# A state-space convolution followed by a gated FFN: per-block sums of spectrum products, a quadrant tap filter with token-major v, an in-place norm, and a new order of all instructions

## The chip, the cores and the metric

The kernel runs on one core of a Trainium2 chip. The metric is the device time of one execution in microseconds, and the median of the runs is compared.

## What is computed

Two layers on 2048 tokens of 640 features. The first normalizes q, filters k with four taps, multiplies by v, convolves the product causally with a 2048-long filter for each feature (given through an FFT), adds a skip term and gates by q. The second normalizes again and applies a gated FFN of width 1728.

```python
def _A_ref(q, k, v, shift_k, ssm_k, ssm_D):
    k_pad = jnp.pad(k, ((0, 0), (ks - 1, 0), (0, 0)))
    k_shift = sum over t of k_pad[:, t:t + S, :] * shift_k[:, ks - 1 - t]
    kv = k_shift * v
    y = irfft(rfft(kv, 2 * S) * rfft(ssm_k, 2 * S))[:S]      # along the tokens
    y = y + kv * ssm_D
    return q * y

def _B_ref(x, w_gate, w_up, w_down):
    return (silu(x @ w_gate) * (x @ w_up)) @ w_down

h = A_q + _A_ref(_layernorm(A_q), A_k, A_v, A_shift_k, A_ssm_k, A_ssm_D)
out = h + _B_ref(_layernorm(h), B_w_gate, B_w_up, B_w_down)
```

Shapes: S = 2048, D = 640, F = 1728, bfloat16 in and out.

## The kernel before

The tokens are cut into four blocks of 512. The long convolution is done block by block in a spectrum of 512 points: four blocks of the filter are transformed once into `C[0]` to `C[3]`, each block i of kv is transformed into `XH`, and the spectrum `Y[i]` of output block i is the sum of the products of input block j with filter block i - j, for j from 0 to i.

For each token block i the stages are:

- `kvload` and `kv`: k and v are brought in feature-major by transposing DMAs on SP's queue (`kT`, `vT`). For each chunk of 128 features TensorE adds up four taps with diagonal 128x128 weights (`diag`, L551). VectorE multiplies the PSUM result by `vT` (L557), and five more transposing DMAs bring the product token-major into `kvo`.
- `xfwd`: 32 matmuls against the table `ftab` (L516), evictions on ScalarE (L522), butterflies on VectorE (`bfly`, L504) into `XH`.
- `prod(j, i)`: on VectorE, two halves of two 2560-wide products (L574, L576), a subtraction and an addition 1280 wide (L579, L581), and for j > 0 an addition into `Y[i]` (L584). As soon as `XH` of block j is there, its products with all filters that need it are due, so the four `Y` all live side by side.
- `ln1`: two statistics passes on ScalarE for each quarter of the block (L592, L595), and on GpSimd an addition of epsilon (L598) and a power of -1/2 (L600).
- `inverse`: matmuls against `itab` (L613) from `OS` and `Y`, evicted on ScalarE with the norm's scale (L621); VectorE multiplies by the centred q (L623) and adds q (L626). Statistics of the second norm on ScalarE (L628, L630) and GpSimd (L632, L634), the normalization on VectorE (L636), and a transposing DMA into `hnT`.
- `ffn`: 14 tiles of gate and up matmuls (L657, L658; the last is packed, L667), evictions on ScalarE (L673, L675), the gate product on VectorE (L677), the down projection (L693), the residual on VectorE (L704) and the output DMA.

`ktrans` (L489, L494) and `kfwd` make the filter spectra from `kc`, with a table `ktab` of their own. The weights `GA`, `UA`, `GB`, `UB`, `PK`, `Wd` are loaded once.

Every operation is a task of a `_Graph`. `schedule` walks through time with a cost for each task and picks for each engine the ready task with the lowest key; the keys of the stages are in the table `ORDER`, limits hold the PSUM units in use by each class (four units of two banks). `emit` writes each engine's list in that order, with semaphore waits for the dependences, so on the chip each engine runs a fixed list, in order.

Of the kernel before, what the change touches and what calls it, by code (L numbers as in the profile page):

```python
# [12 lines left out]
P = 128  # L13
LN_EPS = 1e-5
CELL = 32

# [5 lines left out]
class _Task:  # L22
    __slots__ = ("eng", "fn", "cost", "lat", "prio", "deps", "raw", "succ", "npred", "ready", "end",
                 "opens", "tiles", "idx", "clock", "sem", "seq", "nbytes", "after", "key")


class _Pr:

    def __init__(self, key, base, off=0):
        self.key, self.base, self.off = key, base, off  # L30

    def __add__(self, n):
        return _Pr(self.key, self.base, self.off + n)

    def on(self, eng, table):
        return table.get((eng, self.key), self.base) + 0.01 * self.off
# [28 lines left out]
class _Graph:  # L65

    def __init__(self, nc, es, units=4):
        self.nc = nc
        self.es = es
        self.tasks = []  # L70
        self.lastw = {}
        self.readers = {}
        self.units = units
        self.ps = es.enter_context(nc.psum_tensor("ps", [P, 4096], dt.float32))
        self.psb = self.ps[:].bitcast(dt.bfloat16)
        self.order = None
# [26 lines left out]
    def add(self, eng, fn, cost, prio, r=(), w=(), pr=(), pw=(), skip=(), lat=None, nbytes=0, after=()):  # L103
        t = _Task()
        t.eng, t.fn, t.cost, t.prio = eng, fn, cost, prio
        t.lat = lat if lat is not None else {"pe": 200, "act": 190, "dve": 117, "pool": 110, "sp": 2000}[eng]
        t.nbytes = nbytes
        t.deps, t.raw = set(), set()
        t.after = set(after)
        t.opens = None  # L110
        t.tiles = []
        t.seq = len(self.tasks)
        for ap in r:
            for c in self.cells(ap):
                q = self.lastw.get(c)
                if q is not None:
                    t.deps.add(q)
                    t.raw.add(q)
                self.readers.setdefault(c, set()).add(t)
        for ap in w:  # L120
            for c in self.cells(ap):
                q = self.lastw.get(c)
                if q is not None and q is not t:
                    t.deps.add(q)
                    t.raw.add(q)
# [13 lines left out]
        for pt in pr:  # L139
            t.deps.update(pt.writers)  # L140
            t.raw.update(pt.writers)
            pt.users.append(t)
            t.tiles.append(pt)
        t.deps.discard(t)
        t.raw.discard(t)
        for s in skip:
            t.deps.discard(s)
            t.raw.discard(s)
# [3 lines left out]
    def schedule(self, limits, table):  # L152
        self.limits = limits
        for t in self.tasks:
            t.succ = []
            t.ready = 0.0
        for t in self.tasks:
            t.key = t.prio.on(t.eng, table) if isinstance(t.prio, _Pr) else t.prio
            t.npred = len(t.deps | t.after)
            for d in t.deps | t.after:  # L160
                d.succ.append(t)
        engs = ("pe", "act", "dve", "pool", "sp")
        free = {e: 0.0 for e in engs}
        cand = {e: [] for e in engs}
        for t in self.tasks:
            if t.npred == 0:
                cand[t.eng].append(t)
        unit_free = [0.0] * self.units
        unit_by = [None] * self.units
        used = {}  # L170
        left = {}
        self.last_users = {}
        dma_free = 0.0
        order = {e: [] for e in engs}
        glob = []
        total = len(self.tasks)
        while len(glob) < total:
            best = None
            for e in engs:
                cs = cand[e]  # L180
                if not cs:
                    continue
                open_at = None
                if e == "pe":
                    fu = [u for u in range(self.units) if unit_by[u] is None]
                    open_at = min((unit_free[u] for u in fu), default=None)
                lst = []
                for t in cs:
                    a = t.ready
                    if t.opens is not None:  # L190
                        if open_at is None or used.get(t.opens.cls, 0) >= limits.get(t.opens.cls, 99):
                            continue
                        a = max(a, open_at)
                    lst.append((a, t))
                if not lst:
                    continue
                at = max(free[e], min(x[0] for x in lst))
                a, t = min((x for x in lst if x[0] <= at + 1e-6), key=lambda x: (x[1].key, x[1].seq))
                if best is None or at < best[0]:
                    best = (at, e, t)  # L200
            assert best is not None, "schedule stuck"
            at, e, t = best
            cand[e].remove(t)
            if t.opens is not None:
                pt = t.opens
                fu = [u for u in range(self.units) if unit_by[u] is None and unit_free[u] <= at + 1e-6]
                u = min(fu, key=lambda x: unit_free[x])
                pt.unit = u
                used[pt.cls] = used.get(pt.cls, 0) + 1
                left[pt] = len(pt.users)  # L210
                prev = self.last_users.get(u, ())
                t.deps.update(prev)
                unit_by[u] = pt
            free[e] = at + t.cost
            t.end = at + t.cost + t.lat
            if e == "sp" and t.nbytes:
                dma_free = max(dma_free, at + t.cost) + t.nbytes / 340.0
                t.end = dma_free + t.lat
            for pt in t.tiles:
                left[pt] -= 1  # L220
                if left[pt] == 0:
# [3 lines left out]
                    used[pt.cls] -= 1  # L225
                    self.last_users[u] = [x for x in pt.users if x.eng != "pe"]
            for s in t.succ:
                s.npred -= 1
                s.ready = max(s.ready, t.end)
                if s.npred == 0:  # L230
                    cand[s.eng].append(s)
            order[e].append(t)
            t.idx = len(order[e])
            glob.append(t)
        self.order = order
        self.glob = glob
        return max(t.end for t in glob)

    def emit(self, block):
        nc, es = self.nc, self.es  # L240
        sems = {e: es.enter_context(nc.semaphore("s_" + e)) for e in ("pe", "act", "dve", "pool")}
        known = {e: {} for e in ("pe", "act", "dve", "pool", "sp")}
        prog = {e: [] for e in known}
        nd = 0
        for t in self.glob:
# [3 lines left out]
            for d in t.deps:  # L249
                if d.eng == t.eng == "pe":  # L250
                    continue
                key = d.sem if d.eng == "sp" else d.eng
                val = 16 if d.eng == "sp" else d.idx
# [14 lines left out]
            if t.eng == "sp":  # L268
# [3 lines left out]
                prog["sp"].append(lambda e, t=t: t.fn(e).then_inc(t.sem, 16))  # L272
# [3 lines left out]
        for t in self.glob:  # L276
            if t.eng == "sp" and not t.succ:
# [36 lines left out]
    ("dve", "kv0"): 134.7, ("dve", "kv1"): 333.2, ("dve", "kv2"): 36.6, ("dve", "kv3"): 580.7, ("dve", "mul"): 41.9,  # L314
    ("dve", "p00"): 463.5, ("dve", "p01"): 572.5, ("dve", "p02"): 151.9, ("dve", "p03"): 92.4, ("dve", "p11"): 542.8,
    ("dve", "p12"): 631.7, ("dve", "p13"): 91.9, ("dve", "p22"): 92.9, ("dve", "p23"): 668.8, ("dve", "p33"): 92.9,
    ("dve", "res"): 154.9, ("dve", "xf0"): 584.2, ("dve", "xf1"): 579.6, ("dve", "xf2"): 135.2, ("dve", "xf3"): 758.2,
# [468 lines left out]
```

## Time and profile before

The three runs shown took 302.02, 303.7 and 306.11 us; the median is 303.7.

| | |
|---|---|
| span of the profiled execution | 301.8 us |
| TensorE matmul busy | 264.4 us (88%) |
| VectorE busy | 221.2 us (73%) |
| ScalarE busy | 174.0 us (58%) |
| GpSimd busy | 54.6 us (18%) |
| mean granted TensorE clock | 0.970 |
| moved by DMA | 26.91 MB |
| chain that ended last | TensorE 50%, VectorE 28%, ScalarE 12% |

The span runs from the first to the last instruction of the profiled execution. The page names no other time of that execution; the median of the runs is 1.9 us above its span. Busy time is the union of an engine's instructions; the mean of one instruction includes its overlap with the next on the same engine.

### The profile page before, as it was taken

To read this page: it belongs to the slowest core of one execution; us is meant where nothing else is said; L and a number is where in the kernel's file an instruction comes from. 1 tells how busy PE (TensorE), PEld (TensorE's weight loads), DVE (VectorE), ACT (ScalarE), POOL (GpSimd) and SP (SyncE) were. 2 spreads that over 40 slices of the span, in tenths; PEclk is the share of its full clock that TensorE was granted. 3 is DMA by queue.
4 is the path that set the end of the run, shared out by engine and by line. 5 is a ranking of instruction groups with operands and counts; after the bars stand their busy time and mean duration, and the time that the engine had idled before them with its cause. 6 is when DMAs were issued, how large, how long until landed. Compare 5 with 4: busy or idle time off the path is not lost.

```text
span 301.8 us, 3881 instructions
## 1 busy us (share of the span) xinstructions
PE 264.4 (88%) x1515; PEld 144.5 (48%) x1532; DVE 221.2 (73%) x274; ACT 174.0 (58%) x330; POOL 54.6 (18%) x46
## 2 busy tenths in 40 slices
PE   1889879081789999989999999979999999999995
PEld 1556434050234555646445456644445564544563
DVE  3170898988999999999999999899998322212122
ACT  1749999239674764083289843848959803254400
POOL 0000000305279000015000493630301300000000
PEclk9999998867799999999999999999999999999999
DMA  5999891968445015104301200161000250000011
GB/s 171 249 364 218 219 281 21 239 177 213 83 89 174 0 37 124 50 13 87 109 25 31 57 2 22 34 131 77 0 2 1 48 85 22 11 13 0 0 46 43
DMA packets 55076, 26.91 MB, mean 89 GB/s; under 512 B 45265, under 2 KB 54162, under 8 KB 55058
## 3 DMA queue, kind: packets, MB, share of 16 engines
q1 hardware_dynamic: 55058, 26.67, 35.5%
q8 instruction: 12, 0.20, 0.3%
q14 instruction: 6, 0.05, 0.1%
HBM read 13.49 MB, written 2.62 MB: 53 GB/s over the span
## 4 chain that ended last, share of the span: by engine, by line
PE 50%; DVE 28%; ACT 12%; DMA 3%; POOL 3%; SPq 2%; issue 1%
PE ps L658 13%; PE ps L693 13%; PE ps L657 12%; DVE tt L574 5%; PE ps L516 4%; PE ps L613 4%; DVE Y L584 3%; DVE tt L576 3%; ACT KT L494 3%; PE ps L551 2%; DVE xh L704 2%; POOL mv L632 2%; DVE kT L557 2%; DVE tt L581 2%; ACT qo L630 2%; SPq L447 2%
## 5 line engine op out<-in xcount | busy, mean ns | idle before, releaser
L673 ACT ACTIVATE gu<-ps 128x512 bf16<-128x512 f32 (+1 forms) x56 | 33.4, 599 | 55.6 <-PE ps L658 52.3
L693 PE MATMUL ps<-Wd,gu 128*128 128x320 bf16 x448 | 64.9, 299 | 0.1
L658 PE MATMUL ps<-hnT,UA 128*128 128x512 bf16 x140 | 53.1, 379 | 2.7 <-DMA hnT<-qo 2.0
L693 PEld LDWEIGHTS ps<-Wd,gu 128*128 128x128 bf16 x448 | 41.5, 98 | 23.3 <-issue 6.1
L657 PE MATMUL ps<-hnT,GA 128*128 128x512 bf16 x133 | 50.4, 379 | 1.5 <-DVE kT L557 1.5
L658 PE MATMUL ps<-hnT,UB 128*128 128x512 bf16 x120 | 45.5, 379 | 0.3
L598 POOL TENSOR_SCALAR st<-st 128x4 f32<-128x4 f32 x4 | 24.0, 6004 | 108.9 <-ACT qo L595 108.9
L657 PE MATMUL ps<-hnT,GB 128*128 128x512 bf16 x115 | 43.6, 379 | 0.0
L677 DVE TENSOR_TENSOR gu<-gu,ub 128x512 bf16<-128x512 bf16 (+1 forms) x56 | 23.2, 418 | 24.0 <-ACT ub L675 24.0
L675 ACT ACTIVATE ub<-ps 128x512 bf16<-128x512 f32 (+1 forms) x56 | 33.5, 598 | 2.7 <-PE ps L658 2.6
L704 DVE TENSOR_TENSOR xh<-ps,xh 128x640 bf16<-128x640 f32 x16 | 13.1, 821 | 24.9 <-PE ps L693 24.9
L574 DVE TENSOR_TENSOR tt<-XH,C 128x2560 bf16<-128x2560 bf16 x20 | 29.7, 1484 | 0.1
L576 DVE TENSOR_TENSOR tt<-XH,C 128x2560 bf16<-128x2560 bf16 x20 | 29.6, 1481 | 0.0
L621 ACT ACTIVATE qo<-ps,st 128x640 bf16<-128x640 f32 x16 | 12.7, 792 | 28.8 <-PE ps L613 28.8
L551 PE MATMUL ps<-kT,diag 128*128 128x512 bf16 x76 | 19.1, 403 | 9.8 <-DMA kT<-in_A_k_dram 7.6
L516 PE MATMUL ps<-KT,ktab 128*128 128x320 bf16 x128 | 22.6, 333 | 4.8 <-ACT KT L494 4.0
L632 POOL TENSOR_SCALAR mv<-mv 128x1 f32<-128x1 f32 x16 | 10.0, 627 | 75.7 <-ACT qo L630 75.7
L657 PEld LDWEIGHTS ps<-hnT,GA 128*128 128x128 bf16 x140 | 13.7, 98 | 20.7 <-DMA hnT<-qo 2.1
L658 PEld LDWEIGHTS ps<-hnT,UA 128*128 128x128 bf16 x140 | 13.7, 98 | 15.8
L516 PE MATMUL ps<-kvo,ftab 128*128 128x320 bf16 x128 | 19.5, 300 | 0.0
L516 PEld LDWEIGHTS ps<-KT,ktab 128*128 128x128 bf16 x128 | 12.5, 107 | 13.7 <-ACT KT L494 5.2
L613 PE MATMUL ps<-OS,itab 128*128 128x320 bf16 x64 | 11.2, 335 | 8.6 <-DVE OS L504 8.6
(57 smaller groups left out, 367.1 us busy)
## 6 DMA issues: line engine op xcount, KB each, us to landing
kc<-in_A_ssm_k_dram SPq DMA_DIRECT2D x4, 640.0 KB, 7.1
xh<-in_A_q_dram SPq DMA_DIRECT2D x4, 640.0 KB, 5.5
out_dram<-xh SPq DMA_DIRECT2D x16, 160.0 KB, 1.8
Wd<-in_B_w_down_dram SPq DMA_DIRECT2D x1, 1280.0 KB, 6.2
GA<-in_B_w_gate_dram SPq DMA_DIRECT2D x1, 1120.0 KB, 6.0
UA<-in_B_w_up_dram SPq DMA_DIRECT2D x1, 1120.0 KB, 6.3
GB<-in_B_w_gate_dram SPq DMA_DIRECT2D x1, 960.0 KB, 5.4
UB<-in_B_w_up_dram SPq DMA_DIRECT2D x1, 960.0 KB, 5.2
```

What stands on the lines that cost most here:

```text
L516: last = e.matmul(pt.f(c, W), tab[:, cs, j, f * P:(f + 1) * P], src[:, j, c * W:(c + 1) * W], start=(j == js[0]), stop=(j == js[1]))
L551: last = e.matmul(pt.f(b, N), diag[:, c0 + b, u, :], kT[:, c0 + b, 16 - u:16 - u + N], start=(u == 0), stop=(u == 3))
L574: g.add("dve", lambda e, x=x, k=k: e.tensor_tensor(out=t1, in0=x, in1=k, op=ALU.mult), cdve(2560), prio, r=[x, k], w=[t1])
L576: g.add("dve", lambda e, x=x, k=ksw: e.tensor_tensor(out=t2, in0=x, in1=k, op=ALU.mult), cdve(2560), prio, r=[x, k], w=[t2])
L598: g.add("pool", lambda e: e.tensor_scalar(out=s[:, 2, :], in0=s[:, 1, :], scalar1=LN_EPS * D, scalar2=None, op0=ALU.add), 3000, prio, r=[s ...
L613: last = e.matmul(pt.f(c, W), itab[:, cs, f, j, :], src[:, f, cs, c * W:(c + 1) * W], start=(f == 0 and cs == 0), stop=(f == 1 and cs == 1))
L657: e.matmul(pt.f(0, N), wg[:, c, f0:f0 + P], hnT[:, c, :], start=(c == 0), stop=(c == NC5 - 1))
L658: last = e.matmul(pt.f(1, N), wu[:, c, f0:f0 + P], hnT[:, c, :], start=(c == 0), stop=(c == NC5 - 1))
L673: g.add("act", lambda e, pt=pt, gv=gv, a=ps_g: e.activation(out=gv, in_=pt.f(a[0], N, a[1]), func=ACTF.Silu, scale=D ** 0.5), cact(N), pri ...
L675: g.add("act", lambda e, pt=pt, uv=uv, a=ps_u: e.activation(out=uv, in_=pt.f(a[0], N, a[1]), func=ACTF.Copy, scale=D ** 0.5), cact(N), pri ...
L677: g.add("dve", lambda e, uv=uv, gv=gv: e.tensor_tensor(out=gv, in0=gv, in1=uv, op=ALU.mult), cdve(N), _Pr("mul", -2), r=[gv, uv], w=[gv])
L693: last = e.matmul(pt.f(c, W), slots[fb][0:k, j * P:(j + 1) * P], Wd[0:k, fb, c * W:(c + 1) * W], start=(fb == 0 and not onpe), stop=(fb == ...
```

## The change

The helper classes and the emission stay. What differs:

- The order. Costs and keys no longer decide: `ORDER` holds, for each engine, the written-out list of task numbers, and `schedule` only replays it, hands out PSUM units and sets the semaphores.
- Products. There is one `Y`; `XH` is kept for all blocks. `prod(0, i)` to `prod(i, i)` of block i are tasks of block i (with `prod(0, 3)` ahead of block 3's transform), and the last butterfly writes `IE` and `IO` for the inverse. Filter transforms use `ftab` (no `ktab`), with a `KO` for each block.
- Taps. Chunks 0 to 3 go by quadrants: 64x64 diagonal weights `dg` at four positions of the array, two chunks in one PSUM tile; in the second of the two banks the halves are swapped. Chunk 4 keeps 128x128 weights `dl`. ScalarE evicts the taps, the five transposing DMAs bring them token-major, and v is loaded token-major without a transpose (`vt`) and multiplied there by three VectorE operations that undo the swap.
- Norm. GpSimd makes three values for each token: the square root of the variance sum, its inverse and mean times inverse. ScalarE normalizes q in place; the inverse's eviction adds the square root, and one VectorE multiplication takes the place of L623 and L626. The mean that is missing from q is put back in the residual (`scalar_tensor_tensor` with a scalar).
- The skip term is added to the first tap of the filter (`dcol`) instead of a row of `KT[0]`. The packed last FFN tile writes the lower half of a buffer `gz` whose upper half is zero, so the down projection has no 64-row matmuls.
- Three small loads are issued by ScalarE, q's block 0 is loaded first, and tensors share bytes differently: `kT` with `IO`, `hnT` with `IE`, filter blocks with the FFN buffers and weights.

```diff
-    def schedule(self, limits, table):
+    def schedule(self, order):
...
+        seq = {e: [self.tasks[int(x)] for x in order[e].split()] for e in ENGINES}
...
-        C = [sb("C%d" % m, 10240 * m, [4, 2, D]) for m in range(4)]
-        Y = [sb("Y%d" % i, 40960 + 10240 * i, [4, 2, D]) for i in range(4)]
+        C = [sb("C%d" % m, S[i], [4, 2, D]) for m, i in enumerate((0, 1, 2, 7))]
+        XH = [sb("X%d" % m, S[i], [4, 2, D]) for m, i in enumerate((3, 4, 5, 3))]
+        Y = sb("Y", S[6], [4, 2, D])
+        kT = sb("kT", o + 5120, [NC5, N + 16])
+        IO = sb("IO", o + 5120, [2, 2, D])
+        hnT = sb("hnT", o + 10400, [NC5, N])
+        IE = sb("IE", o + 10400, [2, 2, D])
...
+            load("v%d" % i, vt[:], V2[N * i:N * (i + 1), :].rearrange("(p j) d -> p j d", j=4), 655360)
+            for a in range(3):
...
+                        for t in range(2):
+                            for h in range(2):
+                                s = slice(H * h, H * h + H)
+                                last = e.matmul(pt.f(t, N, slice(H * (h ^ t), H * (h ^ t) + H)), dg[s, c0 + t, u, :], kT[s, c0 + t, x],
+                                                start=(u == 0), stop=(u == 3), tile_position=(H * h, H * (h ^ t)))
...
+                g.add("act", nm, lambda e, pt=pt, ks=ks, nb=nb: e.activation(
+                    out=ks.rearrange("p b (j x) -> p b j x", j=4), in_=pt.f2(N)[:, 0:nb].rearrange("p b (x j) -> p b j x", j=4),
+                    func=ACTF.Copy), cact(N * nb), w=[ks], pr=[pt])
...
+            for lo, src, n, k in ((0, 0, P, 3), (P, P + H, H, 2), (P + H, P, H, 2)):
...
+                g.add("dve", nm, lambda e, a=a, b=b: e.tensor_tensor(out=a, in0=a, in1=b, op=ALU.mult), cdve(4 * n * k), r=[a, b], w=[a])
...
+            g.add("pool", nm, lambda e: e.tensor_scalar(out=s[:, 2, :], in0=s[:, 1, :], scalar1=LN_EPS * D, scalar2=None, op0=ALU.add), 1500,
+                  r=[s[:, 1, :]], w=[s[:, 2, :]])
+            base = s[:, 2:3, :].to_broadcast([P, 2, 4])
+            g.add("pool", nm, lambda e: e.tensor_tensor(out=s[:, 3:5, :], in0=base, in1=half[:], op=ALU.pow), 2500,
+                  r=[s[:, 2, :], half[:]], w=[s[:, 3:5, :]])
+            g.add("pool", nm, lambda e: e.tensor_tensor(out=s[:, 5, :], in0=s[:, 0, :], in1=s[:, 4, :], op=ALU.mult), 1500,
+                  r=[s[:, 0, :], s[:, 4, :]], w=[s[:, 5, :]])
+            for j in range(4):
+                xj = x[:, j, :]
+                g.add("act", nm, lambda e, j=j, xj=xj: e.activation(out=xj, in_=xj, func=ACTF.Identity, scale=s[:, 4, j:j + 1],
+                                                                   bias=s[:, 5, j:j + 1]), cact(D, 2),
+                      r=[xj, s[:, 4, j:j + 1], s[:, 5, j:j + 1]], w=[xj])
...
-                g.add("dve", lambda e, x=x, q=q, s=s, j=j: e.scalar_tensor_tensor(out=q[:], in0=x, scalar=s[:, 0, j:j + 1], in1=q[:],
-                                                                                  op0=ALU.add, op1=ALU.mult),
-                g.add("dve", lambda e, x=x, q=q: e.tensor_tensor(out=x, in0=x, in1=q[:], op=ALU.add), cdve(D), prio + 4,
+                g.add("act", nm, lambda e, pt=pt, q2=q2, s=s, j=j: e.activation(out=q2, in_=pt.f2(W), func=ACTF.Identity, bias=s[:, 3, j:j + 1]),
+                g.add("dve", nm, lambda e, x=x, q=q: e.tensor_tensor(out=x, in0=x, in1=q[:], op=ALU.mult), cdve(D),
...
+                g.add("dve", nm, lambda e, pt=pt, x2=x2, m=m: e.scalar_tensor_tensor(out=x2, in0=pt.f2(W), scalar=m, in1=x2,
+                                                                                    op0=ALU.subtract, op1=ALU.add),
...
         for i in range(1, NB):
+            xload(i)
+            kv(i)
+            ln1(i)
+            if i == 3:
+                prod(0, 3)
+            xfwd(i)
+            for j in range(i == 3, i + 1):
+                prod(j, i)
+            inverse(i)
+            ffn(i)
```

In the written-out order, the first FFN tile stands on TensorE behind 31 of the 32 filter tiles, block 0's transform and inverse, and the taps of block 1. In the changed kernel the gate product is L684, the statistics passes of the first norm are L588 and L591, its GpSimd operations L594, L597 and L599, the in-place norm L603, the inverse's eviction L629 and its multiplication L631, the normalization L641, the taps L540 (quadrants) and L535, the products with v L555, and the residual L702.

More of the change, by code (lines that the diff above doesn't have):

```diff
@@ L22 @@
 class _Task:
[L23 to L36, printed above, removed]
+    __slots__ = ("eng", "fn", "cost", "lat", "deps", "after", "succ", "npred", "ready", "end", "start",
+                 "opens", "tiles", "idx", "clock", "sem", "seq", "dma", "name", "gap")
 class _Tile:
@@ L111, in add @@
         t.tiles = []
+        t.gap = 0.0
         t.seq = len(self.tasks)
@@ L168, in schedule @@
+        assert sorted(t.seq for e in ENGINES for t in seq[e]) == list(range(len(self.tasks)))
+        assert all(t.eng == e for e in ENGINES for t in seq[e])
+        at = {e: 0 for e in ENGINES}
+        free = {e: 0.0 for e in ENGINES}
+        count = {e: 0 for e in ENGINES}
         unit_free = [0.0] * self.units
         unit_by = [None] * self.units
-        used = {}
+        last_users = {}
         left = {}
-        self.last_users = {}
-        dma_free = 0.0
-        order = {e: [] for e in engs}
@@ L195, in schedule @@
[L195 to L203, printed above, removed]
+                    if not fu:
+                        continue
+                    s = max(s, min(unit_free[u] for u in fu))
@@ L204, in schedule @@
+                if best is None or s < best[0]:
+                    best = (s, e, t)
+            assert best is not None, "the orders do not fit together"
+            s, e, t = best
+            at[e] += 1
+            t.gap = s - free[e]
+            t.start = s
             if t.opens is not None:
                 pt = t.opens
-                fu = [u for u in range(self.units) if unit_by[u] is None and unit_free[u] <= at + 1e-6]
-                u = min(fu, key=lambda x: unit_free[x])
+                u = min((u for u in range(self.units) if unit_by[u] is None), key=lambda u: unit_free[u])
@@ L219, in schedule @@
+            t.end = s + t.cost + t.lat
+            if t.dma is not None:
+                pipe = max(pipe, s + t.cost - t.dma[1]) + t.dma[0]
+                t.end = max(pipe, s + t.cost) + t.lat
+            else:
+                count[e] += 1
+            t.idx = count[e]
             for pt in t.tiles:
@@ L425, in bass_sequential_preLN__ssm_conv_h3__swiglu_ffn__prompt_kernel @@
+        mv = [sb("mv%d" % i, o + 320 + 32 * i, [4], f32) for i in range(4)]
+        assert o + 448 <= SBB + 16481 - A0, o + 448
         g = _Graph(nc, es)
@@ L563, in xfwd, with kfwd @@
-        def xfwd(i, prio):
-            halves(kvo, ftab, "xf", XH, OS, 1.0, prio, prio)
+                        g.add("act", name, lambda e, pt=pt, d=d: e.activation(out=d.rearrange("p (b x) -> p b x", b=2), in_=pt.f2(W),
+                                                                             func=ACTF.Copy, scale=scale), cact(D), w=[d], pr=[pt])
+        def kfwd(m, dst):
+            halves("kf", "kf%d" % m, KT[m], dst, KO[m], D ** 0.5 / N)
+            for f in range(2):
+                bfly("kf%d" % m, dst[:, f], KO[m][:, f], dst[:, f], dst[:, f + 2], 2 * D)
@@ L615, in mm @@
                     return last
-                g.add("pe", mm, cpe(W, 8), prio, r=[itab[:], src], pw=[pt])
+                g.add("pe", nm, mm, cpe(W, 8), r=[itab[:], src], pw=[pt])
+                pts.append(pt)
+            for j in range(4):
+                pt = pts[j]
                 x, s = xh[i % 2][:, j, :], st1[i % 2]
@@ new lines, in ffn @@
+                od = O2[N * i:N * (i + 1), :].rearrange("(p j) d -> p j d", j=4)[:, j, :]
+                g.add("sp", "out%d" % i, lambda e, x=x, od=od: e.dma_start(od, x), 350, r=[x], dma=(475, 0), lat=1000)
+        kload(0)
+        kv(0)
+        ktrans(0)
+        kfwd(0, C[0])
+        for m in (1, 2, 3):
+            kload(m)
+            ktrans(m)
+        kfwd(1, R1)
+        kcomb(C[1], R1, C[0], 1)
+        kfwd(2, C[2])
+        kfwd(3, C[3])
+        kcomb(C[3], C[3], C[2], 3)
+        kcomb(C[2], C[2], R1, 2)
```

552 lines of the change are left out of this document (238 added, 314 removed), and 44 rows, old and new, of the table ORDER.

## The prediction

> **What bounds the kernel now.** I read the busy slices first, then the three stretches they fall into, then the groups by shape, and last the timeline around the points where one stretch ends and the next begins.
>
> ```profile
> PE   1889879081789999989999999979999999999995
> DVE  3170898988999999999999999899998322212122
> ACT  1749999239674764083289843848959803254400
> PEclk9999998867799999999999999999999999999999
> ```
>
> A slice is 7.5 us. TensorE has holes in slices 6 to 10 and none that count later; VectorE is full from slice 7 to 28. The stretches, with the busy time of each engine in the middle columns:
>
> ```profile
> core 0: us, PE busy (x) PEld busy (x) DVE busy (x) ACT busy (x) POOL busy (x), PEclk, DMA share, GB/s
> 0.00:84.50 84.50, 54.45 (x338) 31.36 (x342) 60.26 (x62) 57.44 (x100) 8.58 (x16) 0.90 0.79 200
> 84.50:225.30 140.80, 137.00 (x756) 72.88 (x767) 138.81 (x174) 86.98 (x173) 42.31 (x22) 1.00 0.23 57
> 225.30:301.80 76.50, 72.92 (x423) 40.27 (x425) 22.13 (x41) 29.62 (x58) 3.66 (x8) 0.99 0.11 26
> ```
>
> The front (to 84.5) is a chain of dependences: no engine is full over it. The middle is two engines at once, TensorE 97% and VectorE 99%. The end is TensorE alone. A gain in the front counts whole; in the middle both engines must shrink, or the other one holds the time.
>
> ```profile
> 84.48 0.39 PE L657 MATMUL ps<-hnT,GA 128*128 128x512 bf16 x1 [1.50 <-DVE kT L557]
> 85.23 11.18 POOL L598 TENSOR_SCALAR st<-st 128x4 f32<-128x4 f32 x1 [7.94 <-ACT qo L595]
> 89.22 0.41 DVE L677 TENSOR_TENSOR gu<-gu,ub 128x512 bf16<-128x512 bf16 x1
> 94.83 1.48 DVE L536 TENSOR_TENSOR C<-C,R 128x2560 bf16<-128x2560 bf16 x1
> 96.35 1.49 DVE L574 TENSOR_TENSOR tt<-XH,C 128x2560 bf16<-128x2560 bf16 x1
> 96.49 2.25 POOL L600 TENSOR_TENSOR st<-st,half 128x4 f32<-128x4 f32 x1
> 225.33 1.25 PE L613 MATMUL ps<-OS,itab 128*128 128x320 bf16 x8
> ```
>
> The three anchors are the first FFN matmul (84.48), the first gate product on VectorE (89.22) and the last block's inverse transform (225.33). The GpSimd row of L598 is the odd one: a 128x4 operation takes 11.18 us and ends at 96.41, just after VectorE's first pause (a 2560-wide step is 1.40 start to start, so 96.23 to 96.35). It waited for that pause.
>
> ```profile
> L551 PE MATMUL ps<-kT,diag 128*128 128x512 bf16 x76 | 19.1, 403 | 9.8 <-DMA kT<-in_A_k_dram 7.6 <-DVE kT L557 1.9 <-issue 0.2
> L557 DVE TENSOR_TENSOR kT<-ps,vT 128x1024 bf16<-128x1024 f32 x8 | 9.6, 1215 | 1.0 <-PE ps L551 1.0
> L574 DVE TENSOR_TENSOR tt<-XH,C 128x2560 bf16<-128x2560 bf16 x20 | 29.7, 1484 | 0.1
> L623 DVE SCALAR_TENSOR_TENSOR qo<-xh,st,qo 128x640 bf16<-128x640 bf16 x16 | 13.9, 877 | 1.6 <-ACT qo L621 1.6
> L693 PE MATMUL ps<-Wd,gu 64*128 64x320 bf16 x32 | 7.1, 301 | 0.0
> ```
>
> The mean of one includes overlap with the next. I count start to start from the timeline: VectorE 1.402 us for 2560 wide, 0.736 for 1280, 0.336 for a gate product, 0.402 for L626, 0.796 for L623, 0.356 for L636, 0.734 for L704; ScalarE 0.584 for a 640 eviction, 1.118 for 1280, 0.72 and 0.82 for the two statistics passes, 0.49 for an FFN eviction; TensorE 0.216 per 512 columns and 0.136 per 320.
>
> **The front.** In the changed order all but one of the 32 filter tiles still stand ahead of the first FFN tile, so "filter blocks late" moves little of TensorE's work. What leaves the front is VectorE work: products of block 0 with later filters, L557 (reading PSUM) and L623. Its work ahead of the first gate product falls from 59.7 us (28 of 1280, 15 of 2560, 9 of L557, small ones) to 43.4 (29, 10, and six cheap SBUF products). So the front passes to ScalarE. Its queue up to the last statistics pass of block 0: 29 spectrum evictions 16.9, 8 filter transposes 8.9, 5 tap evictions 4.1 (estimate, on the line through 640 and 1280), 16 statistics passes 12.3, 4 in-place norms at 0.73 (L595's activation) 2.9, 4 inverse evictions 2.7: 47.8. The q block is issued first and lands at about 5 (the first filter block took 4.74 from issue to landing), so ScalarE can end at 52.8. It also waits: for the five transposes of kv that start after the tap evictions (1.27 each on SP) and for block 0's products and butterflies before its inverse. I add 5: 58. From there the kernel before took 6.0 (last pass ends 74.98, last hnT lands 81.01), so the first FFN matmul comes at 64.5, not 84.5.
> Costed at nothing here: three small loads on ScalarE's queue (0.4 to 0.5 each) under the wait for q, and v loaded plainly (0.45 on SP for 3 to 5 of a transpose). The new map puts kT on the bytes of IO, so block 1's kT transpose waits for the first inverse tiles, near 46.5, and v, GA, half of PK and the hnT transposes queue behind it on SP: 5 for the transpose, 1 to issue, 6 to land (the page's GA row) gives GA at 58.5. It is hidden by 6 us.
>
> **The middle, VectorE.** The last normalization of block 0 (61.5) is followed by 10.3 us of older work, so the first gate product comes at 72. From it to the second butterfly of the last inverse stand 48 of 2560 (67.3), 57 of 1280 (42.0), 37 gate products (12.4), 8 L631 at L626's time (3.2), 8 L641 (2.8), 8 residual adds with a scalar at 0.80, between L704 and L623 (6.4), 6 token-major products (3.1): 137.2. Before, the like stretch summed to 133.6 and took 136.8, so I add 3.3: 212.5. Gathering the products in one Y leaves the count of additions at 12; it only moves them to their own block, which is why this stretch grows.
>
> **The middle, TensorE.** 39 gate/up tiles of 10 matmuls 84.1, 24 spectrum tiles 13.0, two down projections 30.4, 8 inverse tiles 8.7, three packed tiles 3.2, one filter tile 0.5, two tap blocks. A tap block was 20 matmuls of 0.216 (4.3); now it is 32 quadrant passes and 4 full ones. No row shows quadrants. If four run together it is 2.6; one after another 7.8 (L693's 64-row matmuls, no shorter than full ones, say a part of the array is no cheaper by itself); with every weight load of 0.098 bare 11.3. It cannot be below 2.6. The rows nearest in form, L693's, run in a common tile and say nothing of overlap; the four passes of a tap use different rows or columns of the array and different outputs, so I take 3.0, near the low end. Sum 146; before, 135.1 of such work took 140.9, so I add the same 5.7: 64.5 + 146 + 5.7 = 216.2. TensorE is the later of the two by 4.
>
> **GpSimd.** Each block's norm now has three GpSimd operations, and ScalarE's in-place norm waits for them with FFN evictions queued behind it; before, only a late eviction waited. Between the last statistics pass and the norm stand 6 evictions (block 1) or 9 (blocks 2, 3), 6.5 to 9.7 us at TensorE's pace. In the new VectorE order hardly any instruction waits for the one just before it, so the pause that freed L598 is rarer. When ScalarE stops, VectorE soon lacks gate inputs and pauses, so the loss ends itself. Best 0, worst (11.2 + 2.25 + 2.25, less cover) 9.2 + 6 + 6 = 21; I take 2, because L598 took only 1.24 and 0.79 in the other two blocks.
>
> **The end.** From the last inverse: 13 gate/up tiles 28.0, one packed 1.1, two down projections 30.4, inverse 4.3, tail 3.1 (298.68 to 301.8): 67; before 74.5 of such work took 76.5, so 68. Sum: 216.2 + 2 + 68 = 286.2 against the span of 301.8. The median of the runs is 1.9 above that span, and I add it: 288.
>
> **Rivals.** *Quadrants in pairs.* Passes through the upper and lower rows that write one bank exclude each other: 16 x 0.216 + 0.86 = 4.3 a block, 1.3 more than I took, four times: 293. Nothing in the trace speaks for or against it. The Trainium skill, TensorEngine Tiling (Array Packing), Restrictions and Gotchas, says that different row tiles cannot access the same PSUM bank simultaneously, and here the two halves of a chunk do share a bank; by that rule the time is this rival's.
> *GpSimd starved.* All three norms wait as L598 did at 85.23 and at 170.37 (10.82). With VectorE running dry after some 7 to 10 us and 4.5 for the other two, about 4 of each block is bare: 298. For it: two of four rows. Against: L600 ended at 98.74 while VectorE ran without a pause. The Trainium skill, SBUF — State Buffer, SBUF: two separate sides, has the shared port pair as an exclusive lock held for a whole instruction; by it all three operations would wait, and L600's row does not agree.
> *The front's cover gone.* The kT transpose took up to 9.1 to land, and weights and hnT sit behind it: first FFN matmul at 72, total 296.
> *Slower.* The quadrant passes run one by one with bare weight loads, 11.3 a block: 8.3 more for two blocks in the middle, about 5 for two in the front: 315. It turns the change into a loss of 2% from 8.5 us a block. Against it: 98 ns loads hide under matmuls everywhere in the trace.
> *Nothing lost.* Both engines lose nothing in the middle: 280.
>
> **Chances.** The forecast 0.52 (281 to 294), pairs 0.12, starved 0.15, cover gone 0.08, slower 0.07, nothing lost 0.06. A measurement here tells about 2% from no change: under 297.6 faster, over 309.8 slower. Most of the first two, half of the next two and the last are faster: 0.77; same 0.15; slower 0.08. The range 277 to 302 leaves out the slower case and the edges.
>
> **What would show it.** First FFN matmul at 60 to 69 (right), 75 or more (wrong). First gate product 7 to 8 later. A tap block of chunks on TensorE under 3.5 (right), near 4.3 (pairs), 7 or more (slower). The last inverse at 213 to 223. GpSimd rows of over 8 us with ScalarE waiting on them at the in-place norm mean the starved case. TensorE idle in the middle of more than 12 us would make the sum wrong, wherever it comes from.

## The result, and the profile after

The changed kernel took 300.06 us (median of 6 runs, 299.19 to 300.77), the kernel before 303.56 in the same comparison (6 runs, 301.84 to 306.11): a ratio of 0.989, 95% interval 0.984 to 0.993. It is 1.1% faster where 5.1% had been forecast, and within the 2% that the prediction counts as the same. The profiled execution took 299.81 us, 2.0 above its span of 297.8.

Three rows of the busy slices of the page (a slice is now 7.4 us), TensorE, GpSimd and the granted clock:

```profile
PE   0495978689999499999999899999993999999995
POOL 1003000440009300900007337100592030000000
PEclk9999799799999989999999999999996899999999
```

TensorE has two new holes, in slices 14 and 31 (counted from 1). GpSimd is busy just ahead of both, and the clock is low in or just behind them. The same three stretches as before the change, cut at the first FFN matmul and at the last block's inverse:

```profile
core 0: us, PE busy (x) PEld busy (x) DVE busy (x) ACT busy (x) POOL busy (x), PEclk, DMA share, GB/s
0.00:66.84 66.84, 44.36 (x338) 26.96 (x341) 37.34 (x47) 56.32 (x92) 10.48 (x19) 0.95 0.74 208
66.84:228.15 161.31, 148.41 (x854) 79.29 (x867) 146.70 (x183) 109.19 (x212) 48.71 (x25) 0.98 0.26 65
228.15:297.80 69.65, 66.22 (x388) 39.02 (x391) 19.52 (x37) 29.52 (x56) 3.17 (x8) 0.97 0.11 29
```

The front fell from 84.5 to 66.8 and the end from 76.5 to 69.7. The middle grew from 140.8 to 161.3: TensorE's busy time there rose by 11.4 (137.0 to 148.4), close to the 10.9 by which the forecast's list had grown, and its idle time from 3.8 to 12.9. Some 7.5 us of it are gate and up matmuls that stood in the end before (35 fewer there), about 3 came from the front (the taps of one more block, 12 spectrum matmuls), and 1.7 are no added work but a lower clock, as the first experiment shows. Rows of the timeline around the holes (start, duration, engine, line; in brackets the idle time before and what ended it):

```profile
11.51 1.79 PE L479 MATMUL ps<-ident,kc 128*128 128x128 bf16 x15 [11.51 <-DVE kc L468]
66.84 0.38 PE L662 MATMUL ps<-hnT,GA 128*128 128x512 bf16 x1 [0.56 <-issue]
88.86 8.32 POOL L594 TENSOR_SCALAR st<-st 128x4 f32<-128x4 f32 x1 [25.18 <-ACT jk L591]
97.12 0.83 DVE L489 TENSOR_TENSOR IO<-Y 128x1280 bf16<-128x1280 bf16 x1
97.27 2.22 POOL L597 TENSOR_TENSOR st<-st,half 128x8 f32<-128x8 f32 x1
99.80 1.73 ACT L603 ACTIVATE xh<-xh,st 128x640 bf16<-128x640 bf16 x2 [5.62 <-POOL st L599]
102.52 0.42 DVE L684 TENSOR_TENSOR gu<-gu,ub 128x512 bf16<-128x512 bf16 x1 [4.58 <-ACT ub L682]
102.63 3.92 PE L618 MATMUL ps<-IO,itab 128*128 128x320 bf16 x16 [4.01 <-ACT ub L682]
158.55 5.30 POOL L594 TENSOR_SCALAR st<-st 128x4 f32<-128x4 f32 x1 [31.73 <-ACT jk L591]
211.95 11.60 POOL L594 TENSOR_SCALAR st<-st 128x4 f32<-128x4 f32 x1 [24.58 <-ACT jk L591]
225.62 0.92 ACT L603 ACTIVATE xh<-xh,st 128x640 bf16<-128x640 bf16 x1 [6.64 <-POOL st L599]
228.15 1.22 PE L618 MATMUL ps<-IO,itab 128*128 128x320 bf16 x4 [4.88 <-ACT ub L682]
```

Read it as a chain. The addition of epsilon (L594, 128x4) takes 0.23 us in block 0, where VectorE is idle, but 8.32, 5.30 and 11.60 in the other blocks. A hole on VectorE is here a moment between two records in which neither runs; otherwise each starts a little before the last has ended. In block 1 the addition ends at 97.18, right where VectorE makes its first hole: L489 starts at 97.12, 1.51 behind a 2560-wide step that takes 1.40. In block 2 it ends at 163.85, behind a hole of 0.03 at 163.75, and in block 3 when VectorE has run dry. ScalarE's in-place norm (L603) waits for GpSimd, the FFN evictions stand behind it in ScalarE's queue, VectorE gets no gate inputs (4.58), and TensorE, with no free PSUM, stops for 4.01 and 4.88.

Two theories were open. *Starved*: the missing 12 us is this chain. *Slack*: the stalls fall into time that the middle has to spare, and its list of work, or the front, is what was sized wrongly.

### The profile page after: what moved, and what is told of

Same layout as the page of the kernel before. It is cut to its first block, busy times and chain, and to the rows that moved or that the text cites. A ratio compares the mean times of both kernels' runs of the same rounds, so it can differ in the third digit from the quotient of the medians.

```text
span 297.8 us, 4019 instructions
## 1 busy us (share of the span) xinstructions
PE 259.0 (87%) x1579; PEld 145.3 (49%) x1596; DVE 203.6 (68%) x265; ACT 195.0 (66%) x358; POOL 62.4 (21%) x52
## 4 chain that ended last, share of the span: by engine, by line
PE 36%; ACT 23%; DVE 18%; POOL 14%; DMA 5%; issue 2%; SPq 0%; ACTq 0%
PE ps L696 11%; PE ps L663 9%; POOL st L594 8%; PE ps L662 8%; PE ps L500 5%; PE ps L618 3%; DMA dcol<-in_A_ssm_D_dram 3%; DVE tt L568 3%; DVE tt L569 3%; ACT xh L603 3%; POOL mv L637 2%; ACT KO L506 2%; ACT KT L484 2%; DMA kvo<-kT 2%; POOL st L597 2%; ACT gu L680 2%
## 5 line engine op out<-in xcount | busy, mean ns | idle before, releaser
L594 POOL TENSOR_SCALAR st<-st 128x4 f32<-128x4 f32 x4 | 25.5, 6363 | 104.3 <-ACT jk L591 104.3
L680 ACT ACTIVATE gu<-ps 128x512 bf16<-128x512 f32 x52 | 30.1, 596 | 25.4 <-PE ps L663 25.2
L684 DVE TENSOR_TENSOR gu<-gu,ub 128x512 bf16<-128x512 bf16 x52 | 21.3, 420 | 34.6 <-ACT ub L682 22.6
L682 ACT ACTIVATE ub<-ps 128x512 bf16<-128x512 f32 (+1 forms) x56 | 32.9, 599 | 12.4 <-PE ps L663 6.1
L569 DVE TENSOR_TENSOR tt<-X,C 128x2560 bf16<-128x2560 bf16 x20 | 29.7, 1483 | 0.1
L568 DVE TENSOR_TENSOR tt<-X,C 128x2560 bf16<-128x2560 bf16 x20 | 29.6, 1482 | 0.1
L637 POOL TENSOR_SCALAR mv<-mv 128x1 f32<-128x1 f32 x16 | 13.2, 826 | 77.0 <-ACT qo L635 77.0
L500 PE MATMUL ps<-vt,ftab 128*128 128x320 bf16 x128 | 20.8, 312 | 4.5 <-DVE vt L555 3.5
L500 PE MATMUL ps<-KT,ftab 128*128 128x320 bf16 x128 | 22.0, 320 | 2.6 <-ACT KT L484 1.8
L603 ACT ACTIVATE xh<-xh,st 128x640 bf16<-128x640 bf16 x16 | 14.5, 923 | 14.4 <-POOL st L599 14.4
L702 DVE SCALAR_TENSOR_TENSOR xh<-ps,st,xh 128x640 bf16<-128x640 f32 x16 | 13.8, 877 | 12.8 <-PE ps L696 12.8
L506 ACT ACTIVATE X<-ps 128x640 bf16<-128x640 f32 x16 | 10.8, 703 | 15.9 <-PE ps L500 15.9
L618 PE MATMUL ps<-IO,itab 128*128 128x320 bf16 x64 | 12.1, 352 | 10.2 <-ACT ub L682 8.9
L489 DVE TENSOR_TENSOR C<-C,KO 128x1280 bf16<-128x1280 bf16 x12 | 9.5, 816 | 14.5 <-ACT C L506 14.5
```

Source lines behind the costliest of these rows:

```text
L500: last = e.matmul(pt.f(c, W), ftab[:, cs, j, f * P:(f + 1) * P], src[:, j, c * W:(c + 1) * W], start=(j == par), stop=(j == par + 2))
L568: g.add("dve", nm, lambda e, x=x, k=k: e.tensor_tensor(out=t1, in0=x, in1=k, op=ALU.mult), cdve(2560), r=[x, k], w=[t1])
L569: g.add("dve", nm, lambda e, x=x, k=ksw: e.tensor_tensor(out=t2, in0=x, in1=k, op=ALU.mult), cdve(2560), r=[x, k], w=[t2])
L594: g.add("pool", nm, lambda e: e.tensor_scalar(out=s[:, 2, :], in0=s[:, 1, :], scalar1=LN_EPS * D, scalar2=None, op0=ALU.add), 1500, r=[s[: ...
L603: g.add("act", nm, lambda e, j=j, xj=xj: e.activation(out=xj, in_=xj, func=ACTF.Identity, scale=s[:, 4, j:j + 1], bias=s[:, 5, j:j + 1]), ...
L618: last = e.matmul(pt.f(c, W), itab[:, cs, f, j, :], src[:, f, cs, c * W:(c + 1) * W], start=(f == 0 and cs == 0), stop=(f == 1 and cs == 1))
```

## The experiments

Each kernel is the changed one with one edit, shown by its main lines (`...` stands for the rest); the numbers in `ORDER` are tasks in the order in which the engine runs them. Ratios are to the kernel before, run on the same chip.

**Two pauses by exchange.**

```diff
 ORDER["dve"]
-  ... 361 364 363 246 366 365 ...
+  ... 361 364 366 363 246 365 ...
-  ... 746 618 723 748 614 ...
+  ... 746 748 618 723 614 ...
```

> Two pairs of VectorE instructions stand in another order, so that right after the last statistics pass of blocks 1 and 3 an instruction follows the one whose result it needs (366 behind 364, 748 behind 746). Nothing is added or removed, and block 2 stays as it is. Theory A (GpSimd's addition of epsilon gets in only when VectorE pauses, and ScalarE's in-place norm with the evictions behind it waits for it): in block 1 the addition takes about 3 us instead of 8.32, in block 3 under 1 instead of 11.60; ScalarE's waits of 5.62 and 6.64 shrink to under 2 and to nothing, TensorE's 4.01 and 4.88 ahead of the inverse go, and the time falls by 6 to 9 us to 291 to 294; block 2's 5.30 stays. Rival B (the stalls only take up slack, and the middle is bound by its list of work): the two rows shrink, but the time stays within 2 us of 300. Rival C (the addition does not wait for VectorE's pause but for something else): rows of 8 and 11 us stay.

Measured 287.06, ratio 0.945 (0.941 to 0.950). GpSimd's rows and the three stretches:

```profile
89.04 3.05 POOL L594 TENSOR_SCALAR st<-st 128x4 f32<-128x4 f32 x1 [25.70 <-ACT jk L591]
152.95 5.30 POOL L594 TENSOR_SCALAR st<-st 128x4 f32<-128x4 f32 x1 [31.73 <-ACT jk L591]
206.37 0.63 POOL L594 TENSOR_SCALAR st<-st 128x4 f32<-128x4 f32 x1 [24.58 <-ACT jk L591]
0.00:66.81 66.81, 42.23 (x338) 26.04 (x341) 37.49 (x47) 56.41 (x93) 10.47 (x19) 0.97 0.74 208
66.81:218.06 151.25, 146.70 (x854) 78.57 (x866) 146.44 (x183) 109.73 (x212) 33.68 (x25) 1.00 0.28 70
218.06:285.40 67.34, 63.92 (x388) 38.19 (x391) 19.50 (x37) 28.36 (x54) 3.15 (x8) 1.00 0.11 30
```

Not one instruction was added or removed, and the span fell by 12.4, to 285.4, more than the 6 to 9 that the starved theory had been given. Blocks 1 and 3 are freed; block 2, left alone, still shows its 5.30. The fall is larger than the two holes in TensorE: 8.35 is idle time in the middle (12.90 against 4.55), and 1.7 in the middle and 2.3 at the end are the same matmuls running faster. The granted clock (the column behind POOL) in the four microseconds that start with the inverse, changed kernel first, then this one:

```profile
102.60:106.60 4.00, 3.92 (x16) 2.36 (x18) 4.00 (x6) 2.96 (x6) 0.00 (x0) 0.57 0.00 0
228.10:232.10 4.00, 3.96 (x16) 2.20 (x17) 2.61 (x6) 3.90 (x7) 0.00 (x0) 0.50 0.00 0
```

```profile
98.60:102.60 4.00, 3.95 (x25) 2.41 (x25) 4.00 (x7) 3.35 (x7) 0.00 (x0) 1.00 0.04 9
218.00:222.00 4.00, 3.94 (x29) 2.85 (x30) 3.19 (x7) 3.53 (x6) 0.00 (x0) 1.00 0.00 0
```

After a hole of 4.01 and 4.88 us TensorE ran at about half its clock. The Trainium skill, TensorE: Matmul & The Clock Gate (Part 1), puts the array at half rate after an idle window of about 3.4 us and back after a busy one; the 0.57 and 0.50 agree.

**The norm later in ScalarE's queue.**

```diff
 ORDER["act"]
-  ... 253 327 325 260 261 265 268 269 398 ...
+  ... 253 260 261 265 268 269 327 325 398 ...
-  ... 448 503 504 571 505 579 455 587 ...
+  ... 448 455 503 504 571 505 579 587 ...
-  ... 640 694 644 628 629 693 636 637 648 692 649 645 695 770 ...
+  ... 640 644 628 629 636 694 637 648 693 649 645 692 695 770 ...
```

> ScalarE's in-place norm of blocks 1 to 3 stands a few FFN evictions later in ScalarE's queue (5, 1 and 4 evictions); GpSimd and VectorE are not touched. Theory A: evictions are no longer stuck behind the wait, VectorE and TensorE run on, GpSimd's addition still takes as long or longer, since VectorE has fewer holes, and the time falls by 5 to 9 us to 291 to 295. Rival B (slack): within 2 us of 300. A third possibility: without VectorE running dry, the addition is starved for even longer (over 12 us), and the wait moves to the inverse's evictions: 298 to 304.

Measured 290.79, ratio 0.958 (0.952 to 0.965). GpSimd's addition is held as long as ever (8.33, 5.30, 11.93), yet most of the loss is gone. So a held GpSimd costs little by itself; what costs is who stands behind it in a queue. ScalarE's total wait at the norm fell from 14.4 to 5.1, and the middle took 151.9; what stayed is in the end, 71.5.

**Only one of the two exchanges.** The diffs are the first and the second line of the exchange above.

> Only block 1's exchange (366 behind 364). TensorE stood idle for 4.01 there and the granted clock fell to 0.83 in the 10 us after it; block 3's stall stays as it is. If the two stalls add up to the 13 us of both exchanges by their size: -5 to -6, 294 to 295. Rival (the stall of block 1 is made good later, before block 3): 298 to 300.

> Only block 3's exchange (748 behind 746). TensorE stood idle for 4.88 there, and the granted clock fell to 0.66 in the 10 us after it: -7 to -8, 292 to 293. Rival (the end is bound by something else, such as the last norm's chain): 296 to 299.

Measured 292.52, ratio 0.967 (0.963 to 0.971), and 292.77, ratio 0.969 (0.964 to 0.974). From 0.989 that is 2.2 and 2.0 points, against 4.4 for both, so the two stalls add up within the intervals. Block 1 gave somewhat more than expected, but there 2.2 us are the front (first FFN matmul at 64.68), which the edit does not touch: over the runs whose front is unedited that matmul comes between 64.7 and 66.9, so single profiles of the front differ by some 2 us. The clock of 0.66 behind block 3's stall is the mean from 225 to 235, part of the stall included; from the inverse on (228.1 to 238.1) it is 0.76.

**An explicit pause.**

```diff
+        zz = wcol[:, :, 0:1]
+        for _ in range(6):
+            g.add("dve", "yield", lambda e: e.tensor_tensor(out=zz, in0=zz, in1=zz, op=ALU.subtract), 70, r=[zz], w=[zz])
 ORDER["dve"]
+  863 864 behind 361, 865 866 behind 697, 867 868 behind 746
```

> The changed kernel in its own order, and in each of blocks 1 to 3 two tiny VectorE instructions more (128x5, on a buffer no longer used), the second waiting for the first, placed one or two instructions behind the last statistics pass: a pause and nothing else. Theory (what frees GpSimd is VectorE's pause, not the exchange of two instructions): the addition of epsilon ends at that pause, within 2 to 3 us in all three blocks instead of 8.32, 5.30 and 11.60; ScalarE's waits at the in-place norm go to under 1, block 2's 2.16 too, and the time is 285 to 287 (VectorE pays some 0.3 a block). Rival (the exchanged instructions mattered in another way): rows of 5 us and more, and 293 to 300.

Measured 286.06, ratio 0.945 (0.941 to 0.950). The timeline in block 3:

```profile
205.12 0.65 POOL L594 TENSOR_SCALAR st<-st 128x4 f32<-128x4 f32 x1 [24.58 <-ACT jk L591]
205.58 0.37 DVE L751 TENSOR_TENSOR wcol<-wcol 128x5 bf16<-128x5 bf16 x2
205.85 1.96 POOL L597 TENSOR_TENSOR st<-st,half 128x8 f32<-128x8 f32 x1
205.86 0.42 DVE L684 TENSOR_TENSOR gu<-gu,ub 128x512 bf16<-128x512 bf16 x1
```

The hole between the two tiny instructions is 0.03 us in the records (205.75 to 205.78), and the addition ends at 205.77. It took 1.67, 1.10 and 0.65 in the three blocks, and ScalarE no longer waits at the norm in any of them. The pause is what frees GpSimd, and not what was exchanged.

**Only the addition moved to VectorE.**

```diff
-            g.add("pool", nm, lambda e: e.tensor_scalar(out=s[:, 2, :], ...
+            g.add("dve" if i else "pool", nm, lambda e: e.tensor_scalar(out=s[:, 2, :], ...
```

> Only the addition of epsilon (128x4) of blocks 1 to 3 moves from GpSimd to VectorE, one instruction a block, placed one or two instructions behind the last statistics pass; the power and the multiplication stay on GpSimd. VectorE's order is otherwise that of the changed kernel, with few pauses. Theory A1 (it is this kind of operation that is held while VectorE runs): the power takes 1.7 to 2.9 us though VectorE does not pause, ScalarE's three waits go, also the 2.16 of block 2, and the time is 285 to 288. Rival A2 (any GpSimd operation that comes while VectorE runs without a pause is held): the power's row becomes 5 to 11 us in its place and the time stays at 295 to 300.

Measured 298.18, ratio 0.983 (0.976 to 0.990): A1 fell. The timeline in block 1:

```profile
90.09 0.17 DVE L594 TENSOR_SCALAR st<-st 128x4 f32<-128x4 f32 x1
90.34 8.10 POOL L597 TENSOR_TENSOR st<-st,half 128x8 f32<-128x8 f32 x1 [26.74 <-DVE st L594]
95.44 1.49 DVE L576 TENSOR_TENSOR Y<-Y,tt 128x2560 bf16<-128x2560 bf16 x1
96.97 0.83 DVE L489 TENSOR_TENSOR IO<-Y 128x1280 bf16<-128x1280 bf16 x1
```

On VectorE the addition costs 0.17. Now the power is the first to come, and it is held instead: 8.10, 4.90 and 12.04 us. VectorE's first hole is at 96.93 to 96.97, and the power ends 1.5 later, about its own time (1.67 where VectorE is idle). So both kinds of GpSimd operation that come first here, an addition and a power, are held.

The Trainium skill, SBUF — State Buffer (Who interferes with whom), says that of a VectorE and a GpSimd instruction that need the shared port pair, the one that issues second blocks until the first finishes. By that the hold would be one VectorE instruction, at most 1.49 here; the changed kernel's trace shows it across 8 to 15 of them. The operation right behind a freed one fits better: in the run with the two exchanges the power took 2.88 (207.08), 1.2 more than where VectorE is idle, and a VectorE instruction of 1.49 had started at 206.94.

A hole is not all that ends a hold. The first row below is of the changed kernel, the other two of the kernel before:

```profile
176.04 3.30 POOL L637 TENSOR_SCALAR mv<-mv 128x1 f32<-128x1 f32 x1 [9.85 <-ACT qo L635]
216.43 0.79 POOL L598 TENSOR_SCALAR st<-st 128x4 f32<-128x4 f32 x1 [17.20 <-ACT qo L595]
217.04 1.48 DVE L574 TENSOR_TENSOR tt<-XH,C 128x2560 bf16<-128x2560 bf16 x1
```

The addition of the second norm at 176.04 sees no hole; it ends 0.17 behind the start of L702 (179.17), a VectorE instruction that reads PSUM. The next one with a hold and no hole (181.57, 2.05) ends 0.16 behind such a start too. The row of 0.79 had neither: it came 0.12 behind the start of a VectorE instruction (216.31, 0.82) and ended 0.1 behind its end, while the next one ran on. Why that one waited for a single instruction only is open.

**The skip term left out.**

```diff
-    g.add("dve", "D", lambda e: e.tensor_tensor(out=tap0, in0=tap0, in1=dcol[:], op=ALU.add), 70,
+    g.add("dve", "D", lambda e: e.tensor_tensor(out=dcol[:], in0=dcol[:], in1=dcol[:], op=ALU.add), 70,
```

> The skip term is left out of the computation: the addition of D on VectorE works on D's own buffer, so the first filter transposes no longer wait for D's load (landed at 11.24); the load itself stays. Theory F (D's load is late by itself and on the path): first transposes at 8.1 to 8.5 instead of 11.51, where the identity lands (8.12), ScalarE's idle time of 6.4 us between statistics and first filter eviction shrinks to about 3, the first FFN matmul comes at 64 instead of 66.84, and the time falls by 2.5 to 3.5 us to 297. Rival (hidden later by the kT transpose of block 1, the weights or the order of ScalarE's queue): the first FFN matmul stays at 66 to 67 and the time within 1 us of 300.

Measured 295.27, ratio 0.973 (0.964 to 0.981). The first transposes come at 7.46, when the filter block has landed, the first FFN matmul at 62.82 and the last inverse at 223.91: 4.0 and 4.2 earlier, all of it kept. It is more than expected in part because both the filter block (7.42 for 7.64) and the identity (7.20 for 8.12) landed earlier than in the changed kernel's profile. The time alone is a narrow case (interval 0.964 to 0.981, against 0.984 to 0.993 for the changed kernel); that D is on the path rests on it and on the next three runs together.

**D as a row, with the pauses.** The load of 640 elements of 2 bytes becomes one row of 1280 bytes, added to `KT[0]` on VectorE behind the transposes; the task numbers in `ORDER` shift with it.

```diff
-        g.add("act", "dcol", lambda e: e.dma_start(dcol[:], A_ssm_D.rearrange("(c p o) -> p c o", p=P, o=1), ...
+        drow = qo[3][0:1, :]
+        load("drow", drow, A_ssm_D.rearrange("(o d) -> o d", o=1), 1280, eng="act")
...
+        tap0 = KT[0][0:1, 0, :]
+        g.add("dve", "D", lambda e: e.tensor_tensor(out=tap0, in0=tap0, in1=drow, op=ALU.add), 400, r=[tap0, drow], w=[tap0])
```

> The order of the run with the two pauses, and D as before the change: one row of 1280 bytes in place of 640 elements of 2 bytes, added to the first row of the transposed filter on VectorE, off the path to the transposes. First transposes at about 7.5 instead of 11.0, first FFN matmul at 62.8 (as without the skip term) instead of 66.8, and time 287.06 - 4 = 283, if the two findings add up. If ScalarE's or VectorE's queue takes the gain back in the middle: 285 to 287.

> Both: the addition of epsilon on VectorE, and D as a row. If A1 holds, 281 to 283, no slower than the pauses with the row, since block 2's wait of 2.2 goes as well. If A2 holds, 290 to 296.

> The three explicit pauses and D as one row: if both findings add up as they did with the two exchanges (283.69), 282 to 284; block 2's wait adds at most 1.

With the exchanges 283.69, ratio 0.935 (0.930 to 0.940); with the addition on VectorE 293.59, 0.969 (0.964 to 0.975), as A2 had it; with the explicit pauses 281.80, 0.932 (0.928 to 0.937). The last is the fastest of all: 6.8% below the kernel before, with the whole computation kept. The gains of front and middle add up. In the four runs without D's wait the first FFN matmul comes at 61.4 to 62.8, in the seven with an unedited front at 64.7 to 66.9.

**Full taps, with and without the stalls.**

```diff
-                        for t in range(2):
-                            for h in range(2):
-                                s = slice(H * h, H * h + H)
-                                last = e.matmul(pt.f(t, N, slice(H * (h ^ t), H * (h ^ t) + H)), dg[s, c0 + t, u, :], kT[s, c0 + t, x],
-                                                start=(u == 0), stop=(u == 3), tile_position=(H * h, H * (h ^ t)))
+                        for t in range(2):
+                            last = e.matmul(pt.f(t, N), dl[:, u, :], kT[:, c0 + t, x], start=(u == 0), stop=(u == 3))
```

> Quadrants undone: chunks 0 to 3 go through four full 128x128 matmuls each (20 of 512 columns in a block, 4.3 us at 0.216), as in the kernel before; they all use the weights of chunk 4, and the halves are not swapped, so the computation of the taps is changed. Quadrants run four together (1.92 us for 32 of them in block 0, 0.81 for chunk 4): a block's taps grow by 1.5 us, four blocks 6 us, of which the two in the middle (3.0) and part of the front's show: 303 to 306. Rival (taps are hidden behind ScalarE and VectorE): within 1 us of 300.

> Full 128x128 taps again (chunk 4's weights for all chunks, so the taps are changed), on the order with the two pauses, where TensorE has no stall to hide them in. If TensorE sets the middle, each of the two middle blocks shows 1.5 to 2 us and the front's up to 1: 289 to 291 against 287.06. If VectorE sets the middle (it leads the chain there with 37%), within 1 us of 287.

All chunks use the 128x128 weights of chunk 4 here, so the taps are not those of the filter. Measured 299.05, ratio 0.986 (0.978 to 0.994), where 303 to 306 had been expected, and 288.41, ratio 0.949 (0.944 to 0.955): neither can be told from its partner with quadrants (0.989 and 0.945), and a cost of a microsecond or so can't be excluded. In the second, TensorE is 2.1 us busier in the middle (148.82 against 146.70), and the middle takes 151.48 against 151.25. Quadrants save TensorE 1.7 us a block, a little more than the 1.3 forecast (32 passes in 1.92 where the full ones take 3.62 in block 0), and the kernel nothing that shows: in the middle VectorE is as full as TensorE.

## Why the prediction was wrong

- **The step that failed is GpSimd, the term of 2 us.** It measured 12.4 (297.8 less 285.4), which two pauses took away. The starved rival (298) was what happened. Three parts of the argument broke. Two of the three rows taken as signs that GpSimd usually gets in were special cases: the 1.24 (54.85) ended 0.18 behind the start of L557 (55.91), which reads PSUM, and L600's 2.25 came right behind a freed operation and is still 1.2 longer than its 1.04 in block 0, so it leaves room for a wait of one VectorE instruction, which the prediction read it as speaking against. The third, 0.79, shows that a short wait happens, but among the first norm's first operations it is the only one of its kind in the two profiles. "The loss ends itself" was seen in block 3 alone (VectorE dry at 223.46, the addition over at 223.55), when TensorE's stall of 4.88 had already begun; in block 1 the hole of 0.03 came first, and TensorE still stood for 4.01. And the clock that a stall costs afterwards, some 4 us in middle and end, was in no term. The rival's own working was off too (block 2 cost TensorE hardly anything, and its clock was left out); that its total fitted is partly luck.
- **"Three small loads … costed at nothing" failed as well.** Their cover, the wait for q, ends when q lands at 4.65; D lands at 11.24, and ScalarE, done with its first statistics, stood idle from 8.27 to 12.80. It cost 4.0. That the front still missed by only 2.3 (66.84 for 64.5) is because the 5 us of other waits was some 1.7 too generous: without D's wait it is 62.82. (The terms 58 and 6.0 make 64.0; the 64.5 holds half a microsecond that is not named.)
- **The front's gain was right in kind:** 17.6 of 20 came. The kT transpose's cover held: GA landed at 60.71, 6.1 ahead of its first use. The first gate product came at 75.3, 8.5 behind the first FFN matmul, where 7 to 8 had been given.
- **The middle's sum was right, TensorE's lead was not.** With the pauses the stretch takes 151.25, against 146 + 5.7. But "TensorE is the later of the two by 4" does not hold: 2.1 more of its work changed nothing. A dearer tap block would, by this, have been hidden in part, and the rivals in pairs and one by one were probably priced too high; no run tried more than 2.1. (VectorE's row before the change is full to slice 30 and not 28; nothing rests on it.)
- **Quadrants do run four together:** 32 passes are 6.9 one after another, 3.5 in pairs and 1.7 in fours; they took 1.92 (block 0, and block 1 with the pauses). In the changed kernel's own profile block 1's took 3.45, at a granted clock of 0.54. The Trainium skill's rule that row tiles cannot share a PSUM bank at one time (TensorEngine Tiling (Array Packing), Restrictions and Gotchas) shows no cost here.
- **The end** took 69.65 for 68; 2.3 of it is the clock behind block 3's stall. By the prediction's own practice (67, and the 2 that the kernel before needed on top of its sum) the term was 69.

Without the two stalls the span is 285.4. The forecast without its term for GpSimd was 284.2, so the other terms came out within 1.2 us, partly since the front's two errors offset each other. What stays open: why a first operation is held across many VectorE instructions where the one behind it waits for about one, why the row of 0.79 was not held, and whether the second norm's additions (L637, up to 3.30) cost anything; that was not tried.

## What to carry to other kernels

Before putting a tiny GpSimd operation ahead of a queue that others need, count how long VectorE runs there without a hole and without an instruction that reads PSUM: that, and not the operation's own time, is what its latency can grow to, and two dependent VectorE instructions in a row at the right place are a remedy for almost nothing. Price a TensorE stall of 4 to 5 us as the stall and about 2 us more at a lower clock (1.7 and 2.3 here). A small load is covered only up to the point where the thing that covers it lands.

## What the runs showed of the hardware that was not expected

A hole of 0.03 to 0.04 us on VectorE let a GpSimd operation in that had been held for 5 to 11 us (additions of 5.30, 8.32 and, in the kernel before, 11.18; powers of 4.90 and 8.10). So did the start of a VectorE instruction that reads PSUM, 0.16 to 0.18 before the end of the held operation (holds of 1.24 to 3.30). A 1.2 KB load in 2-byte pieces took 9.5 us from issue to landing, longer than the 48 KB of the identity on the same queue (6.9). And 2 us of TensorE work more or less in a stretch where TensorE was 97% busy made no difference.
